# A gated feed-forward behind linear attention: one opening row with half of it in plain fp32, turned down products, and one merged attention visit per chunk

## The chip, the cores and the metric

The kernel runs on one core of a Trainium2 chip. The metric is device time in microseconds (us), the median of several runs. The engines are TensorE (PE, its weight loads PEld), VectorE (DVE), ScalarE (ACT), GpSimd (POOL) and SyncE (SP), which issues the loads.

## What is computed

Four sequences of 768 tokens go through linear attention with a decaying state (8 heads of 48), and the result, 3072 rows of 384, through a gated feed-forward of width 1536:

```python
for t in range(S):
    cur = np.einsum('bhd,bhe->bhde', u[None] * kt, vt)
    y[:, :, t] = np.einsum('bhd,bhde->bhe', rt, state + cur)
    state = wt[:, :, :, None] * state + np.einsum('bhd,bhe->bhde', kt, vt)
...
gate = 1.0 / (1.0 + np.exp(-(x @ w_gate)))
val = x @ w_val
return (gate * val @ w_out).astype(np.float32)
```

The three weights come as 64-bit floats.

## The kernel before

The work is cut into 24 *chunks* of 128 tokens (chunk q = 4n + b is part n of sequence b) and six *rows* of four chunks, 512 tokens. The feed-forward width is cut into twelve slices f of 128.

**Attention of a chunk.** VectorE makes the decays with two scans: `prep_k` (lines 321 to 327) and `prep_r` (338, 343). TensorE visits a chunk five times, in plain fp32: `turn_k` transposes k (353) and ScalarE copies it out; `sums` forms what each half of the chunk adds to the state (398), which VectorE adds up in `middle` and `keep`; `scores` (371) forms the products of r and k, and the part of the output that comes from the states (378); VectorE masks the scores, a bank for each of two head groups (384); `mix` applies them to the values (422); `take_y` adds the result to the bonus term of POOL (429, two operations); `turn_x` transposes the output (434), and ScalarE and VectorE split it into a high and a low part, `x` (443, 447).

**Feed-forward.** Each weight slice is joined from its 64-bit words on VectorE (251, 255, 259: one operation each in `w_body`, `w_sign`, `w_tail`) and split into a high and a low part, `w_hi` on ScalarE (264) and `w_lo` on VectorE (267). A product of two fp32 matrices is then three products of parts in the fast fp32r form. For a slice f and a group of chunks, `gate` and `value` (`up`, line 455) are nine products each, three parts by three slices of 128 inputs; `sigmoid` (466), `hidden` (473), `hidden_hi` (477) and `hidden_lo` (481) follow on ScalarE and VectorE; `down` (490) takes the hidden part as the stationary operand and `w_out` as the moving one, 384 columns, three products for each chunk, into one bank for each chunk (`po0` to `po3`). After the last slice each bank is copied (496) into one of two buffers and stored (498).

**Order.** Up to the loop a planner (`Plan`, line 142) lays down all instructions from a table of costs, ranks and rooms: this is the opening. It holds rows 0 and 1, two chunks at a time (256 columns), and the attention of chunks 0 to 11, with the preparation of chunk 12. Then a loop written by hand runs rows 2 to 5, four chunks at a time (512 columns). Three steps of it (three slices f) are a *block*; a block carries the attention of one chunk of the next row, as written in `steps` (588). `down` of a step comes one step later. The last row has no attention beside it. PSUM has eight banks: gate, value, four for `down`, two that the attention visits share.

Of the kernel before, what the change touches and what calls it, by code (L numbers as in the profile page):

```python
# [44 lines left out]
def general(ctx: ExitStack, tc: tile.TileContext, dec, tok, wts, u, out, whi, wlo, ident):  # L45
# [10 lines left out]
    raw, t, full, square = tiles("raw", [P, HW], mybir.dt.int64), tiles("t", [P, HW], I32), tiles("full", [P, HW]), tiles("square", [P, HW])  # L56
# [61 lines left out]
    flat = rows.rearrange("b s e -> (b s) e")  # L118
    with tc.For_i(0, NG) as g:
        nc.sync.dma_start(x, flat[bass.ds(g * C, C)])  # L120
        for k in range(NKT):
            nc.tensor.transpose(out=px[:, k * C:(k + 1) * C], in_=x[:, k * P:(k + 1) * P], identity=ident)
        px3 = px[:, :DM].rearrange("a (k c) -> a k c", c=C)
        nc.scalar.copy(xhi, px3)
        nc.vector.tensor_tensor(out=xlo, in0=px3, in1=xhi.bitcast(F32), op=ALU.subtract)
        for f in range(NFF):
            for s, acc in enumerate((pg, pu)):
                for k in range(NKT):
                    cols = slice(s * DM + k * P, s * DM + (k + 1) * P)
                    for j, (w, a) in enumerate(((wlo, xhi), (whi, xlo), (whi, xhi))):  # L130
                        nc.tensor.matmul(acc[:, :C], lhsT=w[f][:, cols], rhs=a[:, k], start=k == 0 and j == 0, stop=k == NKT - 1 and j == 2)
            nc.scalar.activation(gate, pg[:, :C], AF.Sigmoid)
            nc.vector.tensor_tensor(out=h, in0=pu[:, :C], in1=gate, op=ALU.mult)
            nc.scalar.copy(hh, h)
            nc.vector.tensor_tensor(out=hl, in0=h, in1=hh.bitcast(F32), op=ALU.subtract)
            for j, (a, w) in enumerate(((hl, whi), (hh, wlo), (hh, whi))):
                nc.tensor.matmul(po[:, :DM], lhsT=a, rhs=w[f][:, 2 * DM:], start=f == 0 and j == 0, stop=f == NFF - 1 and j == 2)
        nc.scalar.copy(x, po[:, :DM])
        nc.sync.dma_start(out[bass.ds(g * C, C)], x)
# [50 lines left out]

@with_exitstack
def tile_kernel(ctx: ExitStack, tc: tile.TileContext, dec: bass.AP, tok: bass.AP, wts: bass.AP, u: bass.AP, out: bass.AP):
# [50 lines left out]
    def w_guard(f):  # L243
        sq = p1.tile([P, 3 * DM], F32, tag="sq", name=f"sq{f}")
# [421 lines left out]
```

## Time and profile before

| what | value |
|---|---|
| median of three runs | 611.47 us (610.14 to 612.06) |
| span of the profiled execution | 610.9 us |
| PE busy | 565.5 us (93%) |
| DVE busy | 335.1 us (55%) |
| ACT busy | 201.5 us (33%) |
| POOL busy | 97.4 us (16%) |
| first wide product of the opening | 37.57 us |
| first product of the loop | 250.63 us |
| first product of the last row | 524.00 us |

The profile gives the time of one execution from its first to its last instruction (the span). A row names line, engine, operation, output and inputs, shapes and a count; "mean ns" is the mean duration of one instruction, "idle before" the time its engine stood still just ahead, with what ended that. A plain fp32 product appears as two instructions. In timelines the first two columns are start and duration in us.

### The profile page before, as it was taken

Reading aid. Unit: us, or ns where it says so; the run is one execution under the profiler, and the core shown is the slowest. Engines: PE = TensorE matmul, PEld = TensorE weight load, DVE = VectorE, ACT = ScalarE, POOL = GpSimd, SP = SyncE. Lnnn points to the kernel's source line nnn. Section 1 sums busy time; section 2 is a strip of 40 time slices with the busy share of each in tenths; the row PEclk is TensorE's granted clock in tenths of the full one; section 3 lists DMA queues with packets and bytes.
Section 4 is the critical chain, followed back from the end, with each engine's and each line's share of the span. In section 5 each row is a group of like instructions: output and inputs, shape, how many; then the busy total and the mean of one; then the engine's idle time right before and its main releaser. Section 6 shows DMA issues by size and latency. Waiting matters only on the chain. (4 is left out here: it accounts for less than half of the span.)

```text
span 610.9 us, 14604 instructions
## 1 busy us (share of the span) xinstructions
PE 565.5 (93%) x6474; PEld 501.4 (82%) x6474; DVE 335.1 (55%) x570; ACT 201.5 (33%) x402; POOL 97.4 (16%) x86
## 2 busy tenths in 40 slices
PE   4476799999999999699999999999999999999994
PEld 3365799999899999588888888888888888888883
DVE  4989889989686652244644644554554553222220
ACT  3648683444333232212312322212322222321212
POOL 3352121111121411002202202202201210000000
PEclk9998799999999999989999999999999999999997
DMA  8778820033223130122023042022032000100001
GB/s 250 251 315 312 324 86 1 1 86 105 73 94 126 47 125 4 49 85 86 2 86 86 14 124 86 1 85 87 27 111 86 1 1 2 43 11 0 1 2 56
DMA packets 12056, 50.86 MB, mean 83 GB/s; under 512 B 1376, under 2 KB 4576, under 8 KB 10448
## 3 DMA queue, kind: packets, MB, share of 16 engines
q1 hardware_dynamic: 8528, 45.11, 22.8%
q10 hardware_dynamic: 3456, 4.72, 2.2%
q8 instruction: 53, 0.87, 0.6%
q14 instruction: 19, 0.16, 0.1%
HBM read 45.11 MB, written 4.72 MB: 82 GB/s over the span
## 5 line engine op out<-in xcount | busy, mean ns | idle before, releaser
L455 PE MATMUL pg<-x,w 128*128 128x256 f32 (+1 forms) x864 | 174.0, 347 | 1.3 <-DVE w L267 1.2
L455 PE MATMUL pu<-x,w 128*128 128x256 f32 (+1 forms) x864 | 172.0, 345 | 0.0
L455 PEld LDWEIGHTS pg<-x,w 128*128 128x128 f32 x864 | 138.1, 194 | 18.1 <-DVE w L267 1.6
L455 PEld LDWEIGHTS pu<-x,w 128*128 128x128 f32 x864 | 137.5, 193 | 17.4
L490 PE MATMUL po<-w,hh 128*128 128x384 f32 x576 | 148.0, 338 | 0.0
L473 DVE TENSOR_TENSOR sg<-pu,sg 128x256 f32<-128x256 f32 (+1 forms) x96 | 53.5, 557 | 149.4 <-PE pu L455 148.2
L490 PE MATMUL po<-w,hl 128*128 128x384 f32 x288 | 101.5, 353 | 7.2 <-DVE hl L481 7.0
L490 PEld LDWEIGHTS po<-w,hh 128*128 128x128 f32 x576 | 105.3, 189 | 0.9
L477 ACT CAST hh<-sg 128x256 fp32r<-128x256 f32 (+1 forms) x96 | 49.2, 512 | 165.1 <-DVE sg L473 164.7
L466 ACT ACTIVATE sg<-pg 128x256 f32<-128x256 f32 (+1 forms) x96 | 46.8, 488 | 155.8 <-PE pg L455 155.0
L314 POOL TENSOR_TENSOR bon<-tok,a 128x384 f32<-128x384 f32 x24 | 35.0, 1457 | 289.3 <-DVE a L310 289.3
L481 DVE TENSOR_TENSOR hl<-sg,hh 128x256 fp32r<-128x256 f32 (+1 forms) x96 | 55.9, 583 | 39.0 <-ACT hh L477 39.0
L490 PEld LDWEIGHTS po<-w,hl 128*128 128x128 f32 x288 | 54.5, 189 | 10.6 <-DVE hl L481 8.6
L303 POOL TENSOR_TENSOR bon<-tok,ub 128x384 f32<-128x384 f32 x24 | 33.4, 1390 | 114.5 <-DMA tok<-tok 66.8
L429 DVE TENSOR_TENSOR bon<-pa,bon 128x192 f32<-128x192 f32 x48 | 15.6, 353 | 37.6 <-PE pa L422 37.6
L348 ACT ACTIVATE junk<-eg 112x1032 bf16<-112x1032 f32 x24 | 25.6, 1067 | 30.4 <-DVE eg L338 30.2
L321 DVE TENSOR_TENSOR_SCAN eg<-pin,ends 112x516 f32<-112x516 f32 x24 | 30.0, 1250 | 5.2 <-DMA pin<-dec 5.2
L384 DVE TENSOR_TENSOR at<-pa,after 128x256 f32<-128x256 f32 x48 | 18.6, 419 | 22.8 <-PE pa L378 22.8
L338 DVE TENSOR_TENSOR_SCAN eg<-pin,heads 112x516 f32<-112x516 f32 x24 | 30.5, 1271 | 0.0
L353 PE MATMUL pk<-ident,pin 112*128 112x112 f32 x96 | 14.7, 279 | 15.1 <-DVE pin L327 10.1
L306 POOL TENSOR_TENSOR bon<-bon,tok 128x384 f32<-128x384 f32 x24 | 27.3, 1135 | 1.7
L422 PEld LDWEIGHTS pa<-tok,at 64*32 64x32 f32 x1536 | 19.7, 112 | 9.2 <-issue 4.8
(58 smaller groups left out, 434.6 us busy)
## 6 DMA issues: line engine op xcount, KB each, us to landing
pin<-dec SPq DMA_DIRECT2D x23, 675.5 KB, 5.0
tok<-tok SPq DMA_DIRECT2D x24, 576.0 KB, 4.6
wraw<-wts SPq DMA_DIRECT2D x12, 1152.0 KB, 11.4
y<-o ACTq DMA_DIRECT2D x24, 192.0 KB, 2.1
pin<-dec SPq DMA_DIRECT2D x1, 448.0 KB, 4.2
pin<-dec SPq DMA_DIRECT2D x1, 227.5 KB, 3.1
ub<-u SPq DMA_DIRECT2D x1, 192.0 KB, 7.1
```

The lines of the kernel that those rows point to most:

```text
L303: nc.gpsimd.tensor_tensor(out=bon[q], in0=tk[q][:, 0:DM], in1=ub, op=ALU.mult)
L306: nc.gpsimd.tensor_tensor(out=bon[q], in0=bon[q], in1=tk[q][:, DM:2 * DM], op=ALU.mult)
L314: nc.gpsimd.tensor_tensor(out=by_head(bon[q]), in0=by_head(tk[q][:, 2 * DM:]), in1=a0, op=ALU.mult)
L321: nc.vector.tensor_tensor_scan(out=e[:, 516:0:-1], data0=t[:, 516:0:-1], data1=ends[:, 516:0:-1], initial=0.0, op0=ALU.mult, op1=ALU.add,)
L338: nc.vector.tensor_tensor_scan(out=e[:, WW:WW + 516], data0=t[:, 0:516], data1=heads[:, 0:516], initial=0.0, op0=ALU.mult, op1=ALU.add,)
L348: nc.scalar.activation(junk, both, AF.Square, accum_out=acc_d[:, q:q + 1])
L455: nc.tensor.matmul(t, lhsT=w[f][:, cols], rhs=x[n][:, a, k, i0 * C:i1 * C], start=k == 0 and j == 0, stop=k == NKT - 1 and j == 2)
L466: nc.scalar.activation(sg, hid["g", n, f, i0], AF.Sigmoid)
L473: nc.vector.tensor_tensor(out=sg, in0=hid["u", n, f, i0], in1=sg, op=ALU.mult)
L477: nc.scalar.copy(hh, hid["s", n, f, i0])
L481: nc.vector.tensor_tensor(out=hl, in0=hid["s", n, f, i0], in1=hid["hi", n, f, i0].bitcast(F32), op=ALU.subtract)
L490: nc.tensor.matmul(po[n, i][:, :DM], lhsT=h[:, c], rhs=w[f][:, 2 * DM:], start=f == 0 and j == 0, stop=f == NFF - 1 and j == 2,)
```

## The change

**The opening** now holds row 0 alone, with the attention of chunks 0 to 7 and the preparation of chunk 8; the loop runs rows 1 to 5 (`R0 = 1`). Row 0 has two groups of two chunks. The first (chunks 0 and 1) uses plain fp32: x and hidden are not split, the joined weights are used as they are, and each slice takes three products for each of gate, value and down instead of nine, nine and six. The joined words stay in place of the low 64-bit halves (`full(f)`, every second word), and the split of slice f, for the second group and the loop, is written later into the room of slice f - 1, after the first group is through with it. The second group is as before, and lags by four slices. `TURNS`, `COMES`, `LAGS`, `ROOM` and some costs of the planner are changed accordingly.

**Down products** are turned: the weight is stationary, hidden moves with 512 columns (256 in the opening), so a step has nine of them instead of twelve, and the output comes out as features by tokens, in three banks. `leave` copies these into one tile and stores it; in the last row VectorE makes one of the three copies.

**Attention in the loop** takes three visits for a chunk. `both(q)` puts scores and sums of chunk q + 1 and states and mixing of chunk q into one visit. It uses three banks: a pair for scores and sums, one for the outputs of both head groups. Since two row parts of TensorE write that one bank, the products of the first head group wait until the last of the second has left, through a no-operation on SP's queue (`relay`). The two masks of a chunk become one VectorE operation, and so do the two output additions.

```diff
-GROUPS = [(0, 0, 2), (0, 2, 4), (1, 0, 2), (1, 2, 4)]
-LAGS = [0, 6.5, 15, 16]
+GROUPS = [(0, 2, True), (2, 4, False)]
+LAGS = [0, 4]
+R0 = 1
...
+        nc.vector.scalar_tensor_tensor(out=word(f, 0), in0=word(f, 0), scalar=29, in1=temp[f], op0=ALU.logical_shift_right, op1=ALU.bitwise_or)
+
+    def full(f):
+        return word(f, 0, F32)
 
     def w_hi(f):
-        w = const.tile([P, 2, 3 * DM], F32R, tag=f"w{f}", name=f"w{f}")
+        w = const.tile([P, 2, 3 * DM], F32R, tag=f"w{f - 1}", name=f"w{f}")
...
+    def section1(q):
+
+        bank["a", q] = att_pair(f"pa{q}")
+        go(scores(q) + sums(q))
+
+    def section2(q):
...
+        go(among(*states(q, bank["y", q])) + among(*mix(q, bank["y", q])))
...
+    def mask(q):
+        att[q] = p1.tile([P, 2, NP, HC], F32, tag="at", name=f"at{q}")
+        found = bank["a", q][:, :, :NP * HC].rearrange("a o (p c) -> a o p c", c=HC)
+        nc.vector.tensor_tensor(out=att[q], in0=found, in1=after.unsqueeze(1).unsqueeze(1).broadcast_to([P, 2, NP, HC]), op=ALU.mult)
...
+    def take_y(q):
+        mine = bon[q].rearrange("a (p o e) -> a o p e", o=2, e=D)
+        nc.vector.tensor_tensor(out=mine, in0=bank["yy", q], in1=mine, op=ALU.add)
...
+            if e:
+                nc.tensor.matmul(t, lhsT=full(f)[:, cols], rhs=whole[n][:, k, spot], start=k == 0, stop=k == NKT - 1)
+                continue
...
+    def down(n, f, i0, i1, e=False):
+        first, last = f == 0 and i0 == 0, f == NFF - 1
+        if first:
+            po[n] = [ps1.tile([P, 512], F32, tag=f"po{j}", name=f"po{n}_{j}") for j in range(NKT)]
+        for j in range(NKT):
+            cols = slice(2 * DM + j * P, 2 * DM + (j + 1) * P)
+            to = po[n][j][:, i0 * C:i1 * C]
+            if e:
+                nc.tensor.matmul(to, lhsT=full(f)[:, cols], rhs=hid["s", n, f, i0], start=first, stop=last, skip_group_check=True)
+                continue
+            hh, hl = hid["hi", n, f, i0], hid["lo", n, f, i0]
+            for i, (h, w) in enumerate(((hh, wlo), (hh, whi), (hl, whi))):
+                nc.tensor.matmul(to, lhsT=w[f][:, cols], rhs=h, start=first and i == 0, stop=last and i == 2, skip_group_check=True)
+
+    def leave(n):
+        o = stage.tile([P, NKT, B * C], F32, tag="o", name=f"o{n}")
+        for j in range(NKT):
+            if n == NC_ - 1 and j == 1:
+                nc.vector.tensor_copy(o[:, j], po[n][j])
+            else:
+                nc.scalar.copy(o[:, j], po[n][j])
+            nc.scalar.dma_start(out[n, j * P:(j + 1) * P], o[:, j])
...
+    def both(q):
+
+        some = q + 1 < NG
+        if some:
+            bank["a", q + 1] = att_pair(f"pa{q + 1}")
+        t = att_bank(f"py{q}")[:, :H * D].rearrange("a (o p e) -> a o p e", o=2, e=D)
+        bank["yy", q] = t
+        spots = [t[:, o] for o in range(2)]
+        ours, weigh = states(q, spots, True), among(*mix(q, spots))
+        theirs, more = (scores(q + 1), sums(q + 1)) if some else ([], [])
+        early, late = (more[0::4] + more[1::4], more[2::4] + more[3::4]) if q + 1 < NG - B else (more, [])
+        final = ours[1].pop()
+        go(among(ours[1], theirs[0::2]))
+        final = final()
+        sync = mybir.DependencyInfo(mybir.DependencyClass.Sync, mybir.DependencyReason.DATA)
+        relay = nc.sync.nop()
+        tc.add_manual_dep(relay.ins, final.ins.name, sync, reason="rows of tiles take turns at a bank")
+        go(among(early, theirs[1::2]))
+        rest = among(ours[0], late)
+        tc.add_manual_dep(rest.pop(0)().ins, relay.ins.name, sync, reason="rows of tiles take turns at a bank")
+        go(rest)
+        go(weigh)
...
-    for n in range(2, NC_):
+    for n in range(R0, NC_):
```

`scores`, `sums`, `states` and `mix` return lists of products, and `among` puts two lists in turn. In the loop `turn_k` of chunk q + 1 stands in the first step of a block, `both(q)` at the end of the second, `turn_x` of chunk q in the third.

Where the rows moved, three places. First TensorE in the opening, at the first wide products; `pg`, `pu` and `po` are the outputs of gate, value and down, `whole` is x unsplit, `raw` the words of a weight, `pk` the transposes of k. Before:

```order
L398 MATMUL pv_1_393<-tok_359,kT_386 48x48
L455 MATMUL pg_0_0_411<-x_233,w_236 128x256 x9
L455 MATMUL pu_0_0_429<-x_233,w_236 128x256 x9
L371 MATMUL pa_0_444<-pin_221 64x64
L371 MATMUL pa_1_445<-pin_221 64x64
```

And now:

```order
L470 MATMUL px_353<-ident,bon_234 128x128 x3
L502 MATMUL pg_0_0_360<-whole,raw_110 128x256 x3
L502 MATMUL pu_0_0_371<-whole,raw_110 128x256 x3
L357 MATMUL pk_378<-ident,pin_290 128x112 x4
L502 MATMUL pg_0_1_383<-whole,raw_219 128x256 x3
L541 MATMUL po_0_395<-sg_0_0_369,raw_110 128x256
L541 MATMUL po_1_396<-sg_0_0_369,raw_110 128x256
L541 MATMUL po_2_397<-sg_0_0_369,raw_110 128x256
```

The first wide products take three instructions each, from the joined words, directly behind the transposes of chunk 1. Second, VectorE in the opening, between chunks 0 and 1; `full` and `temp` are the weight being joined, `w` its split parts, `eg` the decays. Before:

```order
L251 TENSOR_SCALAR full_187<-wraw_113 128x1152
L429 TENSOR_TENSOR bon_124<-pa_0_151,bon_124 128x4x48
L255 SCALAR_TENSOR_TENSOR full_187<-wraw_113,full_187 128x1152
L429 TENSOR_TENSOR bon_124<-pa_1_152,bon_124 128x4x48
L259 SCALAR_TENSOR_TENSOR full_187<-wraw_113,full_187 128x1152
L447 TENSOR_TENSOR x_233<-px_229,x_233 128x3x128
L321 SCALAR_TENSOR_TENSOR eg_238<-pin_179,ends 112x516
```

And now:

```order
L258 TENSOR_SCALAR temp_172<-raw_110 128x1152
L261 SCALAR_TENSOR_TENSOR temp_172<-raw_110,temp_172 128x1152
L465 TENSOR_TENSOR bon_121<-py_174,bon_121 128x2x4x48
L264 SCALAR_TENSOR_TENSOR raw_110<-raw_110,temp_172 128x1152
L325 SCALAR_TENSOR_TENSOR eg_228<-pin_159,ends 112x516
```

The output sum is one operation, the joined words go back into `raw`, and chunk 0 has no low part of x. Third, TensorE in the loop; `pa` is the bank (now the pair) of scores, `py` the bank of outputs, `ready` and `mid` the states, `at` the masked scores. Before, states end one visit and mixing is another:

```order
L378 MATMUL pa_0_3901<-ready_3785,pin_3519 64x48
L378 MATMUL pa_1_3902<-ready_3785,pin_3519 64x48
L378 MATMUL pa_0_3901<-mid_3885,pin_3519 64x48
L378 MATMUL pa_1_3902<-mid_3885,pin_3519 64x48
L455 MATMUL pg_0_7_3937<-x_2412,w_1196 128x512 x9
L422 MATMUL pa_0_3901<-tok_3521,at_3900 32x48
L422 MATMUL pa_1_3902<-tok_3521,at_3900 32x48
```

And now, at the wait for the relay, with the semaphores that a row waits for:

```order
L389 MATMUL pa_1947<-tok_1725,kT_1899 48x48
L376 MATMUL pa_1947<-pin_1697 64x64
L405 MATMUL py_1948<-ready_1719,pin_1486 64x48 [waits SP_sequencer_49]
L389 MATMUL pa_1947<-tok_1725,kT_1899 64x48
L405 MATMUL py_1948<-mid_1891,pin_1486 64x48
```

Sums and scores of the next chunk stand in turn with the states of this one, and the mixing follows in the same visit.

More of the change, by code (lines that the diff above doesn't have):

```diff
@@ L117, in general @@
     pg, pu, po = (bank.tile([P, 512], F32, name=n) for n in ("pg", "pu", "po"))
[L118 to L139, printed above, removed]
@@ L540, in tile_kernel @@
-        add(f"sm{q}", "PE", 0.55, [f"kT{q}", f"tok{q}"], k + 0.15, sums, q, take=["bank", "bank"], give=["kT"])
-        add(f"mid{q}", "DVE" if old else "ACT", 0.36, [f"sm{q}", old and f"fade{q}"], k + 0.12, middle, q, take=["mid"], give=["bank"])
-        add(f"keep{q}", "DVE", 0.36, [f"mid{q}"], k + 0.15, keep, q, give=["bank"])
-        add(f"sc{q}", "PE", 1.1, [f"pr{q}", f"mid{q}"], k + 0.2, scores, q, take=["bank", "bank", "at"], give=["pin"] + ["ready"] * old)
-        add(f"m0{q}", "DVE", 0.42, [f"sc{q}"], k + 0.2, mask, q, 0)
@@ new lines, in tile_kernel @@
+        add(f"mk{q}", "DVE", 0.76, [f"s1_{q}"], k + 0.12, mask, q)
+        add(f"keep{q}", "DVE", 0.36, [f"mid{q}"], k + 0.15, keep, q)
+        add(f"s2_{q}", "PE", 1.3, [f"mk{q}", f"keep{q}"], k + 0.2, section2, q, give=["at", "pin", "mid"] + ["ready"] * old)
+        add(f"y{q}", "DVE", 0.65, [f"s2_{q}", f"b4_{q}"], k + 0.2, take_y, q, give=["pair"])
+        first = q in (2, B) if exact(0) else q % B == 0
+        add(f"tx{q}", "PE", 0.33, [f"y{q}", q % B and f"tx{q - 1}"], k + 0.4, turn_x, q, take=["bank"] + ["x"] * first, give=["bon"])
@@ L555, in tile_kernel @@
+        plain = q < B and exact(q)
+        add(f"xh{q}", "ACT", 0.68, [f"tx{q}"], k, take_x, q, give=["bank"] * plain)
+        if plain:
+            add(f"xl{q}", None, 0, [f"xh{q}"], k)
+        else:
+            add(f"xl{q}", "DVE", 0.56, [f"xh{q}"], k, rest_x, q, give=["bank"])
+        add(f"tok{q}done", None, 0, [f"s2_{q}", f"b4_{q}", q and f"tok{q - 1}done"], k, give=["tok"])
     for f in range(NFF):
@@ L582, in tile_kernel @@
-    for n in range(2):
-        add(f"x{n}done", None, 0, [f"pu{g}_{NFF - 1}" for g in range(len(GROUPS)) if GROUPS[g][0] == n], 0, give=["x"])
+            if not e:
+                add("hh" + name, "ACT", 0.14 + 0.13 * m, ["hm" + name], soon, hidden_hi, *a)
+                add("hl" + name, "DVE", 0.15 + 0.14 * m, ["hh" + name], soon, hidden_lo, *a)
+            add("dn" + name, "PE", up_cost, [("hm" if e else "hl") + name, f and f"dn{g}_{f - 1}", g and f"dn{g - 1}_{f}"], k - 0.5, down, *a, give=["unit"])
@@ L631, in tile_kernel @@
     down(*last.pop())
+    leave(NC_ - 1)
     own.close()
```

364 lines of the change are left out of this document (201 added, 163 removed).

## The prediction

> **What bounds the kernel now.** I read first the busy time of the engines in six stretches cut at the kernel's own stages: the first wide product of the opening at 37.6 us, the start of the loop at 250.6 us, and the start of the last row at 524.0 us. The columns are busy microseconds and (in brackets) instructions of PE, PEld, DVE, ACT and POOL, then the granted clock, the DMA share and GB/s.
>
> ```profile
> 0.00:37.60 37.60, 16.32 (x339) 13.23 (x339) 27.61 (x37) 17.84 (x31) 14.42 (x23) 1.00 0.84 276
> 37.60:75.00 37.40, 29.19 (x383) 26.60 (x383) 33.07 (x49) 26.63 (x48) 8.39 (x7) 0.83 0.85 314
> 75.00:100.00 25.00, 24.36 (x320) 23.42 (x320) 21.33 (x33) 16.07 (x32) 5.62 (x5) 0.99 0.17 54
> 100.00:250.60 150.60, 146.69 (x2057) 140.01 (x2056) 103.75 (x195) 52.09 (x123) 26.03 (x22) 1.00 0.23 69
> 250.60:524.00 273.40, 271.37 (x3010) 230.38 (x3009) 131.81 (x229) 70.53 (x140) 42.98 (x31) 0.99 0.18 56
> 524.00:610.90 86.90, 77.62 (x375) 67.71 (x374) 17.57 (x31) 18.35 (x32) 0.00 (x0) 0.96 0.06 20
> ```
>
> From 75 us on TensorE is the bound: it is busy for 97 to 99 of 100 us until the last row. Before 75 us nothing is: TensorE loses 21 of 37.6 us and then 8 of 37.4 us, while VectorE is busy for 0.73 and 0.88 of the time. So three sums are wanted: when the loop starts, what its blocks cost, and the end. The timeline of one loop block gives the second (start, duration, engine, line, count):
>
> ```profile
> 397.02 2.33 PE L455 MATMUL pg<-x,w 128*128 128x512 f32 x9
> ...
> 399.28 0.75 PEld L422 LDWEIGHTS pa<-tok,at 64*32 64x32 f32 x64 [0.35 <-issue]
> ...
> 400.09 2.37 PE L455 MATMUL pu<-x,w 128*128 128x512 f32 x9
> ...
> 402.30 0.49 PE L434 MATMUL px<-ident,bon 128*128 128x128 f32 x3
> ...
> 402.55 0.42 PE L490 MATMUL po<-w,hl 128*128 128x384 f32 x1
> ...
> 404.73 2.24 PE L455 MATMUL pg<-x,w 128*128 128x512 f32 x9
> ...
> 406.81 2.20 PE L455 MATMUL pu<-x,w 128*128 128x512 f32 x9
> ...
> 408.85 0.33 PE L490 MATMUL po<-w,hl 128*128 128x384 f32 x1
> ...
> 410.96 2.25 PE L455 MATMUL pg<-x,w 128*128 128x512 f32 x9
> ...
> 413.37 2.30 PE L455 MATMUL pu<-x,w 128*128 128x512 f32 x9
> ...
> 415.60 0.55 PEld L398 LDWEIGHTS pv<-tok,kT 64*64 64x64 f32 x32 [0.35 <-issue]
> ...
> 416.20 0.45 PE L490 MATMUL po<-w,hl 128*128 128x384 f32 x1
> ...
> 418.51 0.61 PEld L371 LDWEIGHTS pa<-pin 48*64 48x64 f32 x29 [0.25 <-issue]
> ...
> 419.70 2.33 PE L455 MATMUL pg<-x,w 128*128 128x512 f32 x9
> ```
>
> A block of three steps and one attention chunk runs from 397.02 to 419.70, 22.68 us. The middle step, 404.73 to 410.96, carries no visit and lasts 6.23: gate 2.08, value 2.04, down 2.11. Against it each visit has a price: mixing 3.07 - 2.08 = 0.99, the transposes of x 2.46 - 2.04 = 0.42, the transposes of k 2.41 - 2.08 = 0.33, the sums 2.83 - 2.04 = 0.79, scores and states 3.50 - 2.11 = 1.39. That is 3.92, and 3 x 6.23 + 3.92 = 22.61. Sums, scores and mixing together are 3.17, of which 0.35 + 0.25 + 0.35 is an idle engine on entering.
>
> **The start of the loop.** Before, two rows and twelve chunks lie ahead of it; now one row and eight chunks (and the preparation of the ninth). These rows give the prices: a start, the spacing of products of 256 columns, the start of the loop, the load of a weight, then groups of VectorE up to 250 us.
>
> ```profile
> 37.57 2.29 PE L455 MATMUL pg<-x,w 128*128 128x256 f32 x9
> ...
> 110.93 1.24 PE L455 MATMUL pu<-x,w 128*128 128x256 f32 x9
> 112.01 1.24 PE L455 MATMUL pg<-x,w 128*128 128x256 f32 x9
> ...
> 250.63 2.25 PE L455 MATMUL pg<-x,w 128*128 128x512 f32 x9
> ```
>
> ```profile
> wraw<-wts SPq DMA_DIRECT2D x12, 1152.0 KB, 11.4
> ```
>
> ```profile
> L481 DVE TENSOR_TENSOR hl<-sg,hh 128x256 fp32r<-128x256 f32 x48 | 22.7, 473 | 6.1 <-ACT hh L477 6.1
> L473 DVE TENSOR_TENSOR sg<-pu,sg 128x256 f32<-128x256 f32 x48 | 20.2, 422 | 29.9 <-PE pu L455 28.6 <-ACT sg L466 1.0
> L338 DVE TENSOR_TENSOR_SCAN eg<-pin,heads 112x516 f32<-112x516 f32 x13 | 17.0, 1311 | 0.0
> ...
> L321 DVE TENSOR_TENSOR_SCAN eg<-pin,ends 112x516 f32<-112x516 f32 x13 | 16.6, 1274 | 5.2 <-DMA pin<-dec 5.2
> ...
> L343 DVE TENSOR_TENSOR pin<-pin,eg 112x512 f32<-112x512 f32 x13 | 11.3, 870 | 0.4
> L327 DVE TENSOR_TENSOR pin<-pin,eg 112x512 f32<-112x512 f32 x13 | 9.9, 760 | 0.0
> L384 DVE TENSOR_TENSOR at<-pa,after 128x256 f32<-128x256 f32 x24 | 9.5, 418 | 6.5 <-PE pa L378 6.5
> ...
> L429 DVE TENSOR_TENSOR bon<-pa,bon 128x192 f32<-128x192 f32 x24 | 8.1, 353 | 7.0 <-PE pa L422 7.0
> ```
>
> The first wide product can't come much sooner: it needs chunks 0 and 1, the same chain as before. It no longer waits for the split of the first weights, but that was done beside the chain. I keep 37.6 us.
>
> TensorE after that. A split product of 256 columns takes 1.08 / 9 = 0.12 us. Plain fp32 at full width isn't in the trace with 256 columns. The nearest row is the transposes of x, plain fp32 of 128 columns: three in 0.49 us, each lasting 0.27, so 0.11 apart. The 32 mixing products of a chunk stand in the trace as 64 loads, so a plain product is two passes: 2 x 2 x 0.11 = 0.43 us for 256 columns. The other end is a pass as fast as a split product, 2 x 0.12 = 0.24; the transposes speak against it, and I take 0.43. The exact half is then 12 x 9 x 0.43 = 46 us and the split half 12 x 27 x 0.12 = 39 us. Six chunks at 3.92 are 24 us. Together 109 us. The Trainium skill (Perfetto Trace Analysis, Engine Utilization) counts fp32 in low and high parts as half the full rate, which would be the 0.24; the transposes' 0.11 per 128 columns disagrees. By that figure the exact half would be 26 us and TensorE's rest 89 us.
>
> VectorE over the same time. Before it is busy 27.61 + 33.07 + 21.33 + 103.75 = 185.8 us up to the loop. Of this go 24 products of gate and value (10.1), 36 low parts (17.0), three first and four second halves of a preparation (3 x 2.03 + 4 x 2.18 = 14.8), eight masks (3.3) and eight output sums (2.8): 138 us is left. Merging the two masks and the two output sums of a chunk saves under 0.2 us a pair, and the joined weights now go to every second word; I count both at nothing. Within 37.6 us 27.6 of it is done, as before; 110 us remains, as much as TensorE's 109. As for the weights, 276 and 314 GB/s brought 22 MB in the first 75 us, twelve weights of 1152 KB are 14 MB, and eight chunks come beside them where there were twelve, so I count no wait for them.
>
> So after 37.6 us two engines with equal work alternate in a fixed order. If neither waits the loop starts at 148 us; at VectorE's 0.88 of the second stretch, at 163 us. I take 0.94: 155 us, against 250.6.
>
> **The loop.** It now has sixteen such blocks where it had twelve. Turning the down products makes twelve products (2.11 us) into nine of the gate's form (2.04 to 2.08): 0.06 a step, 0.18 a block. In the opening six of 384 columns become nine of 256, and that is no difference. Sums, scores and mixing become one visit. Two entries go, 0.6 to 0.7; the products themselves are 3.17 - 0.95 = 2.22, so the low end is 2.57. Against that stand two things that no row shows. In the second and third quarter of the visit the sums come four in a row on the same columns of the array, where before neighbours alternated over four parts; twice the time for those two quarters, each about the sums' 0.44, adds 0.9. And the products of the second row group wait for a relay through SP's queue; between the last product that the relay waits for and the one that waits stand sixteen others, 0.4 us or more, so most of it is hidden. The rest of the visit and the next gate are queued behind that wait on TensorE, and on SP's queue the two loads of chunk q+2, which need this visit's products anyway. An uncovered rest of 0.35 (an entry) is the high end: 3.8. Below 2.57 there is nothing to save. I take 3.0, nearer the low end, since 64 loads in 0.75 us (the mixing) show that parts of the array overlap even so. Against the idle 0.25 to 0.35 on entering a visit, the Trainium skill (TensorEngine Tiling, Key Properties) says that a change of tiling mode drains the engine. By that rule mixing, which uses 64x32 parts, still drains once within the visit: 2.9, and the sum the same within 2 us.
>
> A block is then 22.68 - 0.18 - 0.17 = 22.33 us, sixteen 357 us. The first also holds the separate scores and sums of chunk 8, 1.3 us (0.79 and half of 1.39). 359 us; with 2.57 it is 352, with 3.8 it is 371.
>
> **The end.** From the last row's first product to the end it is 86.9 us, 12 x 0.06 = 0.7 less in the products. Then the outputs:
>
> ```profile
> 604.63 0.48 ACT L496 COPY o<-po 128x384 f32<-128x384 f32 x1 [2.26 <-SPq L633]
> 605.14 0.34 ACTq L498 DMA_DIRECT2D y<-o  x1
> 605.58 0.48 ACT L496 COPY o<-po 128x384 f32<-128x384 f32 x1 [0.47 <-SPq L633]
> 606.09 0.66 ACTq L498 DMA_DIRECT2D y<-o  x1
> ```
>
> The third copy waits 2.26 us for one of two buffers. Now one buffer holds all three parts and one copy goes to VectorE, so that wait and one copy with its issue (0.95) go, while copies of 512 columns are a little longer: 3 us less, 83 us.
>
> The sum is 155 + 359 + 83 = 597 us, against a span of 610.9 us, which is within 0.1% of the median of the runs (611.47); I leave it so. Put otherwise: 96 us less opening pays for four more blocks (91 us), and the loop and the end give 8 more.
>
> **Rivals.** *The opening flows.* VectorE and TensorE hardly wait for each other and the merged visit drops to 2.57: 148 + 352 + 83 = 583. For it speaks that in the third and fourth stretch TensorE stays busy for 0.97 behind a busy VectorE; against it, that both are full now. 0.15. *Plain fp32 at half rate,* 0.24 a product: TensorE has 20 us to spare, VectorE's 110 at 0.96 decide, the loop starts at 152: 594. The transposes speak against it: 0.05. *The merged visit saves nothing,* 3.8 us each: 597 + 16 x 0.8 = 610, no change. 0.12. *Slower: the exact products can't be fed.* Their stationary words are now every second word of the joined weights. Loads of 128 packed columns show as 0.19 us; were a load of strided words to take 0.38, a product would be bound by its two loads, 0.76 in place of 0.43. 108 such products add 36 us to TensorE, the loop starts at about 190, and it ends at 632. It decides from the point where a load takes over 0.215 us; from 0.28 the whole is slower than before. The row for it:
>
> ```profile
> L455 PEld LDWEIGHTS pg<-x,w 128*128 128x128 f32 x864 | 138.1, 194 | 18.1 <-DVE w L267 1.6
> ```
>
> No row shows a strided load. 0.10, and 0.05 more for an opening in which both engines keep only 0.8 of the time, 174, so 616. That the change doesn't do what it says is not likely: the order of the instructions shows the plain products and the merged visit.
>
> **How the numbers follow.** The forecast, 590 to 606, has 0.53. A change under 0.3% (1.8 us, about what a measurement can tell here) is 609 to 613. Faster: 0.53 + 0.15 + 0.05 + half of the 0.12 = 0.79. Same 0.06, slower 0.15. The range reaches from the flowing opening, 583, to 613, past the merged visit without gain.
>
> **What would show it.** The first product of 512 columns near 155 us; plain products 0.43 apart; blocks of 22.3 us, and in them one visit of 3.0 us with one idle entry; no wait of a last copy for a buffer. Wrong it is if the loop starts after 168 us, or if blocks are longer than 22.7: then the relay or the order of the parts costs more than the entries did.

## The result, and the profile after

The changed kernel takes 589.31 us (median of four runs, 588.43 to 591.49) against 610.81 us of the kernel before on the same chip: a ratio of 0.9656, 95% interval 0.9631 to 0.9681. Its profiled execution has a span of 588.1 us.

The same cut into stages as for before: first wide product at 33.73 us, loop at 152.95, last row at 503.77. The columns are busy microseconds and (in brackets) instructions of PE, PEld, DVE, ACT and POOL, then granted clock, DMA share and GB/s.

```profile
0.00:33.73 33.73, 12.70 (x303) 10.45 (x303) 23.58 (x27) 15.14 (x27) 12.69 (x22) 1.00 0.96 293
33.73:75.00 41.27, 37.52 (x423) 31.05 (x424) 38.35 (x48) 30.41 (x50) 11.33 (x8) 1.00 0.77 252
75.00:100.00 25.00, 23.92 (x305) 22.21 (x303) 23.45 (x32) 14.83 (x29) 7.42 (x5) 1.00 0.36 127
100.00:152.95 52.95, 51.48 (x792) 47.74 (x790) 47.80 (x74) 19.42 (x41) 9.71 (x10) 1.00 0.26 75
152.95:503.77 350.82, 350.58 (x3893) 288.85 (x3892) 181.27 (x277) 96.53 (x185) 53.39 (x43) 1.00 0.20 62
503.77:588.10 84.33, 76.39 (x336) 62.20 (x334) 18.43 (x32) 17.47 (x29) 0.00 (x0) 0.99 0.06 20
```

The opening is 97.7 us shorter, the loop up to the last row 77.4 us longer (it holds four more blocks), the end 2.6 us shorter: 22.8 us in all, the difference of the spans. Of this some 7.9 us lie in the twelve blocks that both loops have (0.66 each), 2.6 at the end, and the remaining 12.3 in an opening that hands four blocks to the loop. Of these e2, below, puts 4.8 down to the plain fp32; no run moves the row alone. From 75 us on TensorE is as full as before. In the second stretch VectorE is busy for 0.93 of the time, and TensorE now for 0.91, at a granted clock of 1.00; before it was 0.78 at 0.83.

The timeline of TensorE in one loop block (start, duration, line, count; a block goes from 373.03 to 395.05):

```profile
373.03 2.21 PE L505 MATMUL pg<-x,w 128*128 128x512 f32 x9
...
379.61 2.21 PE L505 MATMUL pg<-x,w 128*128 128x512 f32 x9
381.65 2.20 PE L505 MATMUL pu<-x,w 128*128 128x512 f32 x9
383.69 0.62 PE L545 MATMUL po<-hh,w 128*128 128x512 f32 x2
...
385.82 0.25 PE L405 MATMUL py<-ready,pin 48*64 48x48 f32 x1
...
387.59 0.89 PE L418 MATMUL py<-tok,at 64*32 64x48 f32 x64
388.40 2.34 PE L505 MATMUL pg<-x,w 128*128 128x512 f32 x9
390.58 2.21 PE L505 MATMUL pu<-x,w 128*128 128x512 f32 x9
392.63 0.49 PE L470 MATMUL px<-ident,bon 128*128 128x128 f32 x3
392.87 0.71 PE L545 MATMUL po<-hh,w 128*128 128x512 f32 x2
...
395.05 0.62 PE L505 MATMUL pg<-x,w 128*128 128x512 f32 x2
```

It takes 22.02 us, where before took 22.68. Every wide group, down among them, takes 2.04 where nothing stands beside it. The merged visit lasts from 385.82 to 388.40, 2.58 us. Down ahead of it is 0.09 longer (383.69 to 385.82), the gate behind it 0.14 (388.40 to 390.58): 2.81 in all, where the three visits took 3.17. The relay's wait cannot be seen: in the 350.82 us of the loop TensorE stands still for 0.24 in all.

### The profile page after: what moved, and what is told of

It reads as the page before. It is cut to its first block, busy times and chain, and to the rows that moved or that the text cites. A ratio compares the mean times of both kernels' runs of the same rounds, so it can differ in the third digit from the quotient of the medians.

```text
span 588.1 us, 13530 instructions
## 1 busy us (share of the span) xinstructions
PE 552.6 (94%) x6042; PEld 462.5 (79%) x6042; DVE 332.9 (57%) x485; ACT 193.8 (33%) x359; POOL 94.5 (16%) x86
## 4 chain that ended last, share of the span: by engine, by line
PE 81%; DVE 7%; DMA 4%; issue 3%; ACT 2%; POOL 1%; SPq 0%; ACTq 0%; DVEq 0%; POOLq 0%
PE pg L505 23%; PE pu L505 23%; PE po L545 21%; PE py L405 3%; PE py L418 3%; DMA tok<-tok 3%; PE pa L376 2%; DMA ub<-u 1%; PE pk L357 1%; DVE sg L523 1%; PE pa L389 1%; DVE temp L261 1%; DVE raw L264 1%; DVE w L275 1%; PE po L541 1%
## 5 line engine op out<-in xcount | busy, mean ns | idle before, releaser
L505 PE MATMUL pg<-x,w 128*128 128x512 f32 (+1 forms) x648 | 151.4, 377 | 0.2
L505 PE MATMUL pu<-x,w 128*128 128x512 f32 (+1 forms) x648 | 148.2, 373 | 1.1 <-DVE sg L523 1.1
L523 DVE TENSOR_TENSOR sg<-pu,sg 128x512 f32<-128x512 f32 (+1 forms) x84 | 51.6, 614 | 151.8 <-PE pu L505 143.1
L545 PE MATMUL po<-hh,w 128*128 128x512 f32 (+1 forms) x432 | 128.9, 382 | 0.0
L516 ACT ACTIVATE sg<-pg 128x512 f32<-128x512 f32 (+1 forms) x84 | 45.0, 536 | 184.9 <-PE pg L505 175.4
L545 PEld LDWEIGHTS po<-hh,w 128*128 128x128 f32 x432 | 76.7, 189 | 12.7 <-ACT hh L527 0.2
L527 ACT CAST hh<-sg 128x512 fp32r<-128x512 f32 (+1 forms) x72 | 42.1, 584 | 135.1 <-DVE sg L523 135.1
L545 PE MATMUL po<-hl,w 128*128 128x512 f32 (+1 forms) x216 | 80.7, 374 | 0.0
L531 DVE TENSOR_TENSOR hl<-sg,hh 128x512 fp32r<-128x512 f32 (+1 forms) x72 | 49.1, 682 | 42.5 <-ACT hh L527 42.5
L545 PEld LDWEIGHTS po<-hl,w 128*128 128x128 f32 x216 | 40.7, 188 | 8.0 <-DVE hl L531 0.4
```

The source lines that it names most:

```text
L505: nc.tensor.matmul(t, lhsT=w[f][:, cols], rhs=x[n][:, a, k, spot], start=k == 0 and j == 0, stop=k == NKT - 1 and j == 2)
L516: nc.scalar.activation(sg, hid["g", n, f, i0], AF.Sigmoid)
L523: nc.vector.tensor_tensor(out=sg, in0=hid["u", n, f, i0], in1=sg, op=ALU.mult)
L527: nc.scalar.copy(hh, hid["s", n, f, i0])
L531: nc.vector.tensor_tensor(out=hl, in0=hid["s", n, f, i0], in1=hid["hi", n, f, i0].bitcast(F32), op=ALU.subtract)
L545: nc.tensor.matmul(to, lhsT=w[f][:, cols], rhs=h, start=first and i == 0, stop=last and i == 2, skip_group_check=True)
```

## The experiments

All are edits of the changed kernel except the fifth. Times in us; each ratio is to the kernel before as timed beside that run (its median lay between 610.57 and 611.91). The stages are from one profiled execution each, cut at the first product of the loop and of the last row; "a block" is the loop's usual block.

| kernel | median | ratio to before (95%) | span | loop starts | to the last row | to the end | a block |
|---|---|---|---|---|---|---|---|
| before | 610.81 | | 610.9 | 250.63 | 273.37 | 86.9 | 22.69 |
| the change | 589.31 | 0.9656 (0.9631 to 0.9681) | 588.1 | 152.95 | 350.82 | 84.3 | 22.03 |
| e1 two visits | 593.10 | 0.9716 (0.9693 to 0.9739) | 590.6 | 152.86 | 353.46 | 84.3 | 22.18 |
| e2 nothing plain | 597.62 | 0.9780 (0.9758 to 0.9802) | 596.1 | 157.76 | 353.77 | 84.6 | 22.03 |
| e3 bare relay | 597.63 | 0.9780 (0.9748 to 0.9811) | 595.6 | 153.66 | 357.67 | 84.3 | 22.39 |
| e4 sums in turn | 587.75 | 0.9632 (0.9602 to 0.9661) | 586.2 | 153.07 | 348.43 | 84.7 | 21.82 |
| e5 before, turned | 607.26 | 0.9940 (0.9919 to 0.9960) | 606.6 | 250.41 | 271.51 | 84.7 | 22.56 |
| e6 all plain | 599.40 | 0.9806 (0.9781 to 0.9832) | 599.2 | 162.25 | 351.71 | 85.2 | 22.03 |
| e7 together | 584.11 | 0.9557 (0.9537 to 0.9578) | 583.4 | 152.83 | 347.01 | 83.6 | 21.77 |
| e8 nine fillers | 609.34 | 0.9972 (0.9954 to 0.9991) | 607.6 | 168.65 | 354.79 | 84.2 | 22.03 |
| e9 stores back | 585.60 | 0.9571 (0.9549 to 0.9593) | 584.1 | 153.98 | 346.98 | 83.1 | 21.77 |
| e10 less joining | 583.64 | 0.9535 (0.9506 to 0.9564) | 583.3 | 147.37 | 351.53 | 84.4 | 22.03 |
| e11 three fillers | 597.90 | 0.9779 (0.9754 to 0.9804) | 599.1 | 162.91 | 351.25 | 84.9 | 22.03 |

### The merged visit: e1, e4, e3

**e1** cuts it in two again. The second half stands one step later, since scores of q + 1 and outputs of q then share the pair of banks in turn.

```diff
-        at(1, 3, both, q)
+        at(1, 3, section2, q)
...
-            at(1, 3, mask, q + 1)
-            at(1, 3, middle, q + 1)
+            at(2, 1, section1, q + 1)
+            at(2, 1, mask, q + 1)
+            at(2, 1, middle, q + 1)
...
```

> The merged visit is cut in two again: states and mixing of chunk q where it stands now, scores and sums of chunk q + 1 one step later, between gate and value; no relay is needed. Theory A (the prediction's): entering a visit costs 0.30 to 0.35 us of TensorE, so one entry more in each of sixteen blocks makes it 4.8 to 5.6 us longer than after, blocks of 22.35. Theory B (the pitches of after): before a visit the wide product is 0.09 us longer, behind it 0.13, but apart the two halves take 1.065 and 1.426 us as in the opening, 2.49 against 2.58 together. Then the block is 0.1 us longer, 22.1 to 22.2, and the whole 1 to 2.5 us.

The timeline of e1:

```profile
387.52 0.26 PE L405 MATMUL py<-ready,pin 48*64 48x48 f32 x2
...
388.95 2.35 PE L505 MATMUL pg<-x,w 128*128 128x512 f32 x9
391.23 0.69 PE L376 MATMUL pa<-pin 48*64 48x64 f32 x32
...
392.30 2.35 PE L505 MATMUL pu<-x,w 128*128 128x512 f32 x9
```

The halves take 1.43 (387.52 to 388.95) and 1.07 (391.23 to 392.30). The block is 0.15 longer, the loop 2.6 us. That is theory B, just above its end: against this merged visit, cutting it costs half of what the prediction's price of an entry would make it.

**e4** only changes the order in which the sums are taken.

```diff
-        early, late = (more[0::4] + more[1::4], more[2::4] + more[3::4]) if q + 1 < NG - B else (more, [])
+        early, late = (among(more[0::4], more[1::4]), among(more[2::4], more[3::4])) if q + 1 < NG - B else (more, [])
```

> In the second and third quarter of the merged visit the sums alternate between the two column halves of the array instead of coming four in a row on one. Theory A (the prediction's high end): runs on the same columns cost up to 0.9 us a visit, so the visit of 2.58 us comes down to 1.7 to 2.1, 8 to 14 us less. Theory B (the visit takes only 0.09 us more than its halves apart): 0 to 1.4 us less.

The timeline of its visit:

```profile
383.77 0.25 PE L405 MATMUL py<-ready,pin 48*64 48x48 f32 x1
...
385.31 0.88 PE L418 MATMUL py<-tok,at 64*32 64x48 f32 x64
386.12 2.35 PE L505 MATMUL pg<-x,w 128*128 128x512 f32 x9
```

The visit takes 2.35 instead of 2.58; ahead of mixing it is 1.54 instead of 1.77. Runs of four on the same columns did cost, 0.23 us a visit, which lies between the two theories: a quarter of A's upper end and more than B's (2.4 us over the loop). The medians alone don't part e4 from the change, since their intervals overlap; the reading rests on the blocks, of which the usual one takes 21.82 instead of 22.03. Only now does e1 show what an entry is worth. Against e4 the two visits of e1 make a block 0.36 longer, 5.0 us over the loop: 0.14 because the halves take 2.49 apart and 2.35 in turn with each other, the rest in the wide products at their edges.

**e3** takes away the cover of the relay: the products between the last one that it waits for and the one that waits for it come later.

```diff
-        go(among(early, theirs[1::2]))
         rest = among(ours[0], late)
...
         go(rest)
+        go(among(early, theirs[1::2]))
         go(weigh)
```

> The products that stand between the last one of the first row group and the one that waits for the relay (half of the sums and of the scores) come behind the states instead, so nothing covers the relay. Theory A (the relay costs nothing because these products cover it): TensorE idles in each visit for what the relay takes, 0.3 to 0.8 us, 5 to 13 us in sixteen blocks. Theory B (the relay is as quick as the pace of the products): no change, within 1 us.

The timeline at the place of the wait:

```profile
391.49 0.23 PE L376 MATMUL pa<-pin 48*64 48x64 f32 x2
391.83 0.25 PE L405 MATMUL py<-ready,pin 48*64 48x48 f32 x1
391.84 0.25 PE L389 MATMUL pa<-tok,kT 64*64 64x48 f32 x1
```

Products that came 0.06 us apart now stand 0.34 apart. A visit is 2.90 long, a block 0.36 longer, the loop 6.9 us: theory A, at its lower end. So the relay takes about 0.3 us, and the change hides all of it.

### Turning alone: e5

The kernel before, with turned products in its loop; the rest of down stays.

```diff
+        if n >= 2:
+            if f == 0:
+                po[n] = [ps1.tile([P, 512], F32, tag=f"po{j}", name=f"po{n}_{j}") for j in range(NKT)]
+            for j in range(NKT):
+                cols = slice(2 * DM + j * P, 2 * DM + (j + 1) * P)
+                for i, (h, w) in enumerate(((hh, wlo), (hh, whi), (hl, whi))):
+                    nc.tensor.matmul(po[n][j], lhsT=w[f][:, cols], rhs=h, start=f == 0 and i == 0, stop=f == NFF - 1 and i == 2)
...
```

> The kernel before, with one part of the change alone: in the loop's rows 2 to 5 down is turned (nine products of 512 columns into three banks, three copies and stores a row); the opening and the visits stay. Theory A (the prediction's): 0.06 us a step, 48 steps, 2.9 us less than before. Theory B (plain steps of after last 6.12 in place of 6.23): 0.11 a step, 5.3 us less, and a last stretch as before, as the third copy still waits for one of two buffers.

The ratio of 0.994 is 3.7 us (2.4 to 4.9), between the two. The timeline says why:

```profile
395.98 2.34 PE L455 MATMUL pg<-x,w 128*128 128x512 f32 x9
...
403.69 2.21 PE L455 MATMUL pg<-x,w 128*128 128x512 f32 x9
...
409.81 2.21 PE L455 MATMUL pg<-x,w 128*128 128x512 f32 x9
...
418.54 2.33 PE L455 MATMUL pg<-x,w 128*128 128x512 f32 x9
```

A plain step (403.69 to 409.81) takes 6.12, 0.11 less than before, as in the last row of the change: down takes 2.04 instead of 2.11, and the gate behind it 2.04 instead of 2.08. The steps with visits gain 0.01 here, and up to 0.03 in the usual block, which is 0.13 shorter, 22.56. Taken in this order, turning first, 0.13 of the 0.66 that a block of the change is shorter is the turning and 0.53 the visits; no run has the visits without the turning. What the turning also gave is the bank without which the merged visit has no room.

### The opening: e2, e6, e10, e8, e11

**e2** has both groups in split products, with the split of a weight due where its joining is.

```diff
-GROUPS = [(0, 2, True), (2, 4, False)]
+GROUPS = [(0, 2, False), (2, 4, False)]
...
-        add(f"wh{f}", "ACT", 1.15, [f"wt{f}", f and f"wl{f - 1}", f and f"wg{f - 1}", f and f"dn0_{f - 1}"], k + 4, w_hi, f)
+        add(f"wh{f}", "ACT", 1.15, [f"wt{f}", f and f"wl{f - 1}", f and f"wg{f - 1}"], k, w_hi, f)
...
```

> The first group of the opening row is split like the second; nothing is in plain fp32. Theory A (TensorE sets the opening): 12 x 9 plain products of 0.43 become 12 x 27 of 0.12, 7.5 us less, the loop starts at 145 to 148. Theory B (up to 75 us VectorE sets it, busy for 0.93): 12 low parts of hidden (0.52 each) and two of x (0.55) are added and low parts of weights (1.3 to 1.5 each) come sooner, so the loop starts at 153 to 160, no gain and up to 7 us loss.

Its stretches from the first wide product, at 36.28, to the loop:

```profile
36.28:75.00 38.72, 30.40 (x430) 27.96 (x431) 35.06 (x43) 28.11 (x48) 8.72 (x6) 0.82 0.61 216
75.00:100.00 25.00, 24.38 (x339) 23.53 (x338) 23.94 (x37) 17.03 (x33) 3.72 (x3) 1.00 0.52 177
100.00:157.76 57.76, 53.64 (x854) 51.47 (x853) 53.95 (x82) 22.56 (x50) 13.09 (x10) 1.00 0.19 59
```

Theory B: TensorE has less to do (108.4 us behind the first product, against 112.9) and the loop starts 4.8 us later. Half of this is the first product, 2.5 us later, as the transposes of chunk 1 stand behind the transposes of k for the next chunk here. Then TensorE waits, for up to 4.00 us:

```profile
59.65 1.13 PE L376 MATMUL pa<-pin 48*64 48x64 f32 x32 [2.06 <-DVE pin L347]
...
67.81 2.29 PE L505 MATMUL pg<-x,w 128*128 128x256 f32 x9 [4.00 <-DVE w L275]
```

Besides, this execution lost some 3 us within the loop, of which 1.4 stand ahead of one mixing without a cause that the profile names; that part is left open.

**e6** has both groups in plain fp32, and splits the weights behind the second.

```diff
-GROUPS = [(0, 2, True), (2, 4, False)]
+GROUPS = [(0, 2, True), (2, 4, True)]
...
-f and f"dn0_{f - 1}"], k + 4, w_hi, f)
+f and f"dn1_{f - 1}"], k + 8, w_hi, f)
...
```

> Both groups of the opening row are in plain fp32; the weights are split for the loop alone, behind the second group. Theory A (behind 75 us TensorE sets the opening, busy for 0.97): 12 x 27 products of 0.12 become 12 x 9 of 0.43, 7.5 us more, the loop starts at 158 to 161. Theory B (VectorE sets the whole opening): 12 low parts of hidden and two of x go, about 7 us, the loop starts at 146 to 150.

The loop starts at 162.25, 9.3 us later: theory A, a little past its end. Half in plain fp32 is better than none and than all.

**e10** leaves out one operation of the joining, so that the weights are not those of the reference, and VectorE has 9 us less to do.

```diff
-        nc.vector.tensor_scalar(out=t, in0=word(f, 1), scalar1=3, scalar2=0x3FFFFFF8, op0=ALU.logical_shift_left, op1=ALU.bitwise_and)
...
-        nc.vector.scalar_tensor_tensor(out=temp[f], in0=word(f, 1), scalar=-0x40000000, in1=temp[f], ...)
+        nc.vector.scalar_tensor_tensor(out=temp[f], in0=word(f, 1), scalar=-0x40000000, in1=word(f, 1), ...)
...
```

> After, with one of VectorE's three operations that join a weight left out (0.76 us, twelve of them, 9 us; the weights that come out are not those of the reference). TensorE's work is the same. Theory A (VectorE sets the opening up to 75 us): the loop starts 3 to 6 us sooner, at 147 to 150; TensorE's 113 us behind the first product allow no more than 147. Theory B (TensorE alone sets it): 152 to 153.

Its stretches from 33.6 us to the loop:

```profile
33.60:75.00 41.40, 40.35 (x449) 34.56 (x450) 38.54 (x46) 32.12 (x56) 10.01 (x7) 1.00 0.90 297
75.00:100.00 25.00, 24.68 (x368) 22.75 (x367) 24.73 (x36) 16.11 (x30) 8.71 (x6) 1.00 0.19 53
100.00:147.37 47.37, 47.23 (x703) 43.68 (x701) 38.40 (x60) 16.97 (x37) 13.84 (x9) 1.00 0.28 83
```

Theory A: the loop starts 5.6 us sooner, and TensorE has 112.3 us of work in 113.8. VectorE's 9 us were worth 5.6, and then TensorE was full. In the change both are on the path, as the prediction had it.

**e8 and e11** ask whether TensorE's waits in e2 hurt through the slow products behind them. They put nine or three more products ahead of gate and value.

```diff
+        if n == 0 and i0 == 0 and 0 < f < 8:
+            for j in range(9):
+                nc.tensor.matmul(t, lhsT=whi[f - 1][:, :P], rhs=x[n][:, 0, 0, :2 * C], start=j == 0, stop=j == 8)
         for k in range(NKT):
```

> As e2 (nothing in plain fp32), with nine more products of 256 columns ahead of gate and value of slices 1 to 7 of the first group, from weights that are there already; their results are overwritten, and they only fill TensorE's waits. Theory A (up to 75 us VectorE sets the opening, and TensorE's slow products there are a consequence of its waits that costs nothing): the loop starts no sooner than in e2, 157 to 165. Theory B (what costs is that TensorE runs at half rate after its waits): the granted clock is back near 1.00 between 33 and 75 us, and the loop starts at 150 to 155.

> As e8 with three fillers instead of nine ahead of gate and value (0.36 us each, 5 us of TensorE's work in all, less than its waits there). Theory A (VectorE sets the stretch up to 75 us): the loop starts at 157 to 163, not sooner than in e2. Theory B (the half rate behind the waits is what costs): granted clock above 0.95 between 33 and 75 us and a loop start of 151 to 155.

The loop starts at 168.65 and 162.91, later than the 157.76 of e2 by 10.9 and 5.2 us (one profile each; the median of e11 is that of e2). By its time neither run is theory B; e8 lies past the 165 of theory A as well. Not all of this is the fillers': they start at slice 1, and the first product, ahead of any of them, came at 36.92 and 38.66 instead of 36.28, so some 10 and 3 us are left. And the granted clock between 33 and 75 us came only to 0.93 and 0.89, from 0.84 in e2 (the column ahead of the last two), so the condition of theory B was not met. First e8, then e11:

```profile
33.00:75.00 42.00, 34.06 (x405) 31.75 (x406) 35.05 (x43) 25.34 (x45) 9.63 (x8) 0.93 0.64 218
```

```profile
33.00:75.00 42.00, 31.20 (x368) 28.55 (x369) 37.18 (x45) 26.83 (x47) 10.53 (x8) 0.89 0.65 222
```

Fillers delay what is queued behind them and do not close the long waits (4.00 us at most in e2, 2.67 in e8, 3.35 in e11). What the slow products of e2 cost by themselves stays open. Other runs give a hint: e1, e4 and e7 have the change's opening, but in their profiled executions the granted clock fell to half for 3.4 us. In e4 six plain products then take 2.72 us (71.73 to 74.45) where the change's take 1.40 (72.24 to 73.64):

```profile
71.73 2.93 PE L502 MATMUL pg<-whole,raw 128*128 128x256 f32 x6 [0.72 <-DVE raw L264]
74.45 1.72 PE L502 MATMUL pu<-whole,raw 128*128 128x256 f32 x6
```

Yet their loops start at 152.86, 153.07 and 152.83, the change's at 152.95. Such a short stretch cost nothing that can be seen.

### A better version: e7 and e9

**e7** takes e4's order, moves the transposes of x, splits the sums of the bounds from the product that needs them, and issues two of the last three stores from SP.

```diff
...
-        at(2, 2, turn_x, q)
+        at(2, 1, turn_x, q)
...
-            nc.scalar.dma_start(out[n, j * P:(j + 1) * P], o[:, j])
+            (nc.sync if n == NC_ - 1 and j < 2 else nc.scalar).dma_start(out[n, j * P:(j + 1) * P], o[:, j])
...
+                if n == NC_ - 1 and j == 0 and i == 1:
+                    count_bounds()
...
```

> The change with four small edits: the sums in turn as in e4; the transposes of x between gate and value instead of behind value; in the last row two of three stores are issued on SP's queue, so that no copy stands behind the issue of a store; the sums of the bounds go to VectorE a step ahead of the product that waits for them. Theory A (each of these waits is on the path): against after 3 to 4 us for the sums, 0.35 at each of four row starts (1.4 us), about 1 us at the last copy and 0.9 us at the bounds, 6 to 7 us in all, a span of 581 to 583. Theory B (only the order of the sums is on the path): a span of 584 to 586.

These lines of the change were the reason: weights of gate that wait for the last low part of x (four rows share the 1.9 us), the bounds, and the last copies, where ScalarE's third copy stands behind the issue of the second store, which waits for VectorE's copy.

```profile
L505 PEld LDWEIGHTS pg<-x,w 128*128 128x128 f32 x648 | 113.4, 188 | 23.4 <-DVE x L490 1.9
```

```profile
511.31 0.19 PE L564 MATMUL total<-count,ones 128*1 128x1 f32 x2 [0.90 <-DVE count L562]
...
580.39 1.75 ACTq L554 DMA_DIRECT2D y<-o  x2
...
582.18 0.59 ACT L553 COPY o<-po 128x512 f32<-128x512 f32 x1 [1.82 <-issue]
```

The loop is 3.8 us shorter than the change's, 2.4 by e4's order and 1.4 at the row starts; the last row's products are 1.3 us shorter, at its first step. The stores brought nothing that can be seen:

```profile
575.94 0.58 ACT L553 COPY o<-po 128x512 f32<-128x512 f32 x1 [0.82 <-PE po L545]
576.55 0.34 ACTq L554 DMA_DIRECT2D y<-o  x1
```

The last copy no longer stands behind an issue, but 7.5 us pass from the last product (575.90) to the end, where the change took 7.0. That difference is no finding by itself: eight profiles of kernels that end as the change does (e1, e2, e3, e4, e6, e8, e10, e11) have 6.8 to 7.8 there. In all it is 4.7 us by the spans, and 583.4 lies between the two theories: the row starts and the bounds were on the path, the last copy showed nothing, and the sums gave 2.4 us instead of 3 to 4. **e9** puts the stores back:

```diff
-            (nc.sync if n == NC_ - 1 and j < 2 else nc.scalar).dma_start(out[n, j * P:(j + 1) * P], o[:, j])
+            nc.scalar.dma_start(out[n, j * P:(j + 1) * P], o[:, j])
```

> As e7, with all stores of the last row issued by ScalarE again, as in after. Theory A (three stores that leave at about the same time land together, so moving their issue gained nothing): the stretch behind the last product is 7.0 to 7.3 us as in after and e4 instead of 7.5 in e7, a span of 582.5 to 583.4. Theory B (the issue ahead of the last copy is on the path): the last copy starts 1 us later and the span is 584.0 to 584.5.

The last stretch is 7.1 us, as theory A says, and the last row to the end 0.5 shorter than in e7, although the last copy starts 1.47 us behind the last product (578.47, against 577.00) where in e7 it started after 0.04. So a later last copy did not make the end later. But 7.1 and 7.5 both lie within the 6.8 to 7.8 of equal endings, the loop of this execution started 1.1 us later, which the edit does not touch, and the span of 584.1 is theory B's. By their intervals e7 and e9 cannot be told apart; both are faster than the change.

## Why the prediction was right, and where its terms were off

The forecast of 597 lies 7.7 us above the result. The result is within the range of 583 to 613, but just below the band of 590 to 606 that had 0.53, and a little nearer to the rival at 583 than to the forecast. The sum was made of three terms; the loop's is the one that was far off.

**Start of the loop: 155, measured 152.95.** The first wide product came at 33.73, not at 37.6. In before VectorE makes the first half of the next chunk's preparation (31.28 to 33.29) ahead of chunk 1's last output sum, and TensorE takes the next chunk's sums between the transposes of chunk 1 and the first product at 37.57, 3.4 us behind them:

```profile
34.16 0.85 PE L434 MATMUL px<-ident,bon 128*128 128x128 f32 x3
36.10 1.54 PE L398 MATMUL pv<-tok,kT 64*64 64x48 f32 x32 [1.09 <-ACT kT L357]
```

In the change both come later, so the transposes start 2.0 us sooner, and 1.6 us ahead of the product:

```profile
32.16 0.90 PE L470 MATMUL px<-ident,bon 128*128 128x128 f32 x3 [0.75 <-DVE bon L465]
33.73 2.93 PE L502 MATMUL pg<-whole,raw 128*128 128x256 f32 x6 [0.67 <-ACT whole L485]
```

Keeping the old chain was the step that failed there; how much of the 3.9 us the fewer visits brought, and how much the plain fp32, no run separates (e2, with the same visits and all products split, came at 36.28). Behind it TensorE had 112.9 us of work (109 forecast) and VectorE 109.6 (110), in 119.2 us; TensorE's share is 0.947 (0.94 chosen). Most of the 4 us more are the first six plain products, which took 5.28 instead of 2.6. The prediction's own rows had shown it, nine products of 256 columns lasting 2.29 us at 37.57 against 1.24 at 110.93, and it priced all products by the later ones. So the term came within 2 us partly by luck: the first product was 3.9 us sooner, the stretch behind it 1.8 longer. The other plain products were 0.43 apart, as forecast:

```profile
41.02 1.46 PE L541 MATMUL po<-sg,raw 128*128 128x256 f32 x6
42.31 1.46 PE L502 MATMUL pu<-whole,raw 128*128 128x256 f32 x6
```

Three products take 1.29 us. So a plain product costs 0.43, 3.6 times the 0.12 of a split one, and not the 0.24 of the rival at half rate. The Trainium skill (FP8 and Floating Point Precision, TensorE Precision Notes) counts four passes for true FP32; the trace is near that.

The slower rival, products that can't be fed from every second word, did not come. Strided loads take 196 ns and packed ones 191, and two loads stay below the 0.43 us of a product:

```profile
L541 PEld LDWEIGHTS po<-sg,raw 128*128 128x128 f32 x72 | 13.3, 196 | 3.2 <-DVE sg L523 2.1
...
L505 PEld LDWEIGHTS pg<-x,w 128*128 128x128 f32 x110 | 14.1, 191 | 0.1
```

**The loop: 359, measured 350.82.** Blocks take 22.03 and not 22.33, 4.8 us over sixteen. The turning came near (0.18 forecast, 0.13 in e5), but only as a sum: a plain step gains 0.11 instead of 0.06, the two steps with visits next to nothing. The mis-sized term is the visit: 0.17 forecast (3.17 to 3.0), 0.53 measured against e5; in the change's own block, edges included, it takes 2.81. Two entries, with what else the regrouping changes, were worth 0.74 (a block of e5 with three visits against e1 with two: 0.38; e1 against e4 with one: 0.36), near the forecast 0.6 to 0.7. That, too, was luck in part: the 0.25 and 0.35 read as an idle engine are idle times of weight loads, while TensorE's products were busy for 271.37 of the loop's 273.40 us before; what an entry costs shows instead in longer wide products at its edges (2.13 and 2.18 instead of 2.04 in the block above). The counterweights were far too heavy: the runs on the same columns cost 0.23 where 0.9 was the bound, and the relay nothing where 0.35 was. Taking 3.0 out of a range of 2.57 to 3.8, whose upper end nothing in the trace supported, cost 0.3 us a block. Another 2.05 us is a slip in counting: the loop's first step has no down, since down comes one step later. (The visits of chunk 8 in the first block, 0.79 and half of 1.39, add up to 1.5 and not 1.3; 1.2 was measured.) The four blocks of the last loop row with attention, whose last chunks need no final state, take 86.91 instead of 88.1, 1.2 us.

**The end: 83, measured 84.3.** Up to its last product the row takes 77.35 us instead of 78.48, 1.1 less where 0.7 was forecast. Behind it 6.95 pass instead of 8.44, 1.5 less where 3 were counted. The wait for an output buffer went, as forecast, but ScalarE's last copy now waits for the issue of stores (1.82 us where it was 2.26). In e5 the third copy still waits for a buffer:

```profile
601.59 0.59 ACT L495 COPY o<-po 128x512 f32<-128x512 f32 x1 [2.48 <-PEq L646]
```

Even so 7.78 us pass there from the last product to the end, within the 6.8 to 7.8 of the endings without that wait. So the step that failed is to put the whole 2.26 us of a wait on the path to the end. By these profiles at most some 1 us of it was; one profile each can't settle how much.

**Beside the forecast** stood a rival, a flowing opening at 583. The bare visit did come down to 2.58, as that rival had it, and the loop to near its 352, though 2.05 us of that are the slip above. The opening did not reach 148, and e10 shows why: VectorE holds it.

## What to carry to other kernels

When a change moves work between two engines that are both nearly full, sum both and expect the time somewhat above the larger sum, which was 0.947 of it here; then check the split by moving it either way. Here none, half and all in the slower precision gave 157.8, 153.0 and 162.3. Price a visit of small products by the start-to-start times of the wide products on both sides, not by the idle time shown ahead of it: the idle engine overlaps with products that still run. And when small products of several array parts are put into one visit, order them so that neighbours alternate over the parts, and put enough of them between a cross-engine wait and what it waits for; each was worth 0.2 to 0.3 us a visit here.

## What the runs showed of the hardware

- **A wide product behind another kind of product took about 0.13 us longer, also at the same tile size.** The down products behind the transposes of x (128x128, plain fp32) take from 392.87 to 395.05, 2.18, where down alone takes 2.04 (a third of a plain step of 6.12); the gate behind the merged visit takes 2.18 as well. Ahead of the merged visit it is 0.09, ahead of the transposes 0.01. The Trainium skill (TensorEngine Tiling (Array Packing), Key Properties) puts a drain down to a change of tiling mode; at the transposes the mode is the same. Within the merged visit mixing, whose tiles differ from those ahead of it, starts 0.14 us behind the last of these (387.45 to 387.59), where most of those follow each other within 0.06: that fits a drain, but no run tests it.
- **TensorE's products took twice as long while the granted clock stood at half.** In e2 nine products of 256 columns take 2.09 (67.81 to 69.90), and 1.08 elsewhere; the granted clock is 0.50 from 59.2 to 72.8 us. It fell ahead of the wait of 4.00 us, behind one of 0.73 and within one of 2.06. In e4 it fell at 71.6, behind a wait of 1.78 and within one of 0.72; the change's profiled execution has the same waits there and no fall, and its granted clock is 1.00 throughout the opening. The Trainium skill (TensorE: Matmul & The Clock Gate, Part 1) has the array fall to half rate after an idle window of about 3.4 us and back after one that is busy. The half rate agrees; a single wait of that length stands ahead of neither fall. The first six plain products of the change are slow as well (33.73 to 39.01), in a stretch whose granted clock stands as 1.00, so that column does not show every slow product.
- **A relay from TensorE through SP's queue and back took about 0.3 us** (e3: 0.34 us between products that otherwise come 0.06 apart).
